# Sorted block attention into a maxout layer: item 1's query transposes from TensorE to DMA, later value loads, later steps

## The chip, the cores and the metric

The kernel runs on one core of a Trainium2 chip. The metric is the device time of one execution in microseconds (us). Times inside a profile are counted from the span's start; the span runs from the first to the last instruction of the program. In the profile TensorE is PE (its weight loads are PEld), VectorE DVE, ScalarE ACT, GpSimd POOL and SyncE SP.

## The reference

Four items (the batch), each with 8 heads of 768 tokens and head size 64. A head's keys and values are cut into 8 blocks of 96 tokens; a normalized 8 x 8 matrix P per head mixes ("sorts") the blocks; each query block attends to its sorted block; the heads side by side go through a maxout layer.

```python
P = sort_net
for _ in range(5):
    P = P - np.max(P, axis=-1, keepdims=True)
    P = np.exp(P)
    P = P / (np.sum(P, axis=-1, keepdims=True) + 1e-09)
    P = P / (np.sum(P, axis=-2, keepdims=True) + 1e-09)
k_sorted = np.einsum('bhij,bhjcd->bhicd', P, k_b).reshape(B, H, S, D)
v_sorted = np.einsum('bhij,bhjcd->bhicd', P, v_b).reshape(B, H, S, D)
scores = scale * np.matmul(q_b, k_sb.transpose(0, 1, 2, 4, 3))
scores = scores - np.max(scores, axis=-1, keepdims=True)
attn = np.exp(scores)
attn = attn / (np.sum(attn, axis=-1, keepdims=True) + 1e-09)
x = np.matmul(attn, v_sb)     # then the heads side by side: 3072 tokens x 512
out = np.maximum(x @ w1, x @ w2) @ w_out     # 512 -> 1024 -> 512
```

## The kernel before

All inputs are float32 in memory. GpSimd's DMA queue loads them and casts them to bf16 on the way. The maximum is rewritten: w1 becomes w1 - w2, the hidden part is a ReLU of x(w1 - w2), and the product of w2 and w_out, called wc (`w_product`, L654), is added by x. So an output tile of 128 tokens sums 12 matmuls of 512 columns: 8 on the hidden tiles g and 4 on xT.

**Stages.** Item 0's attention runs in a front part whose order is a written list (L777). Then, for each item b in turn, `units` are issued one after the other (L915 to L939): eight `moe_h` (hidden products, 4 for each half of the tokens), and twelve `moe_out` half-tiles of six matmuls, each pair of output tiles ending in one evacuation and one store of 512 KB on SyncE's queue. For item 0 the eight hidden units stand in the front, so its units 0 to 7 are empty, units 8 to 11 are the four `w_product`, and 12 to 23 are the output half-tiles. For items 1 and 2 units 0 to 7 are hidden and 8 to 19 output; item 3 has no attention beside it.

**Tails.** Next item's attention is laid between the units of the current one. The dictionaries `first_tail`, `second_tail` and `third_tail` (L859 to L913) say after which unit which steps are issued. Each engine runs its instructions in the order of issue, so a step that waits holds up all that follows it on its engine.

The steps of item b:
- KS, `sort_k` (L449), three of them: 32 small matmuls each sort keys into PSUM, then an evacuation to kT.
- `q_transposes` (L413), two halves of two head pairs each. For items 0 and 1, 24 TensorE transposes with the identity and one VectorE evacuation a half; for items 2 and 3, a DMA transpose on SyncE's queue out of q_pair, which `pair_q` (L403, two VectorE copies) makes from the loaded queries.
- SC, `scores` (L539), u = 0 to 7: eight matmuls and an exponential on ScalarE. u counts two halves of the blocks times four head pairs, so u = 0, 1, 4, 5 read half 0 of the turned queries and the others half 1.
- TURN, `turn_v` (L242): VectorE turns 24 of 96 columns of the loaded values into v_dc. The values of items 1 and 2 lie in two halves of the partitions and are turned and sorted together.
- VS, `sort_v_pair` (L516, eight of 16 matmuls, items 1 and 2) or `sort_v_halved` (L493, four, item 3, whose values lie in both halves): each reads all turned columns.
- VA, `values` (L567): eight matmuls, a reciprocal and a scaling on VectorE.
- TR, `x_transposes` (L600): for items 1 to 3 a DMA transpose on SyncE's queue, after two VA, into xT. The hidden products of token half 0 read TR0 (their first two matmuls) and TR1 (the next two), those of half 1 TR2 and TR3.

PSUM has four buffers of two banks, shared by all. `pick` (L96) gives an evacuation to ScalarE or VectorE by a running count of their loads, at build time.

**Loads.** All inputs but the small sort matrix are loaded on GpSimd's queue in order of issue; by the trace at most eight are under way, and the ninth waits for the first. The order before: item 0's values, keys, queries; the weights (L822 to L829); keys of 1 (L832), queries of 1 (L836), values of 1 and 2 in two pieces each (L837 to L839), keys of 2 (L840), queries of 2 (L844, into w2's place); values of 3 once turned values are out of v_raw (after unit 11 of item 0); keys and queries of 3 into v_raw's place (after unit 12 of item 1). A tiny GpSimd copy into `seen` (L771, L822) is used to hold that queue back until what it reads is there.

Of the kernel before, what the change touches and what calls it, by code (L numbers as in the profile page):

```python
# [11 lines left out]
BF16 = mybir.dt.bfloat16  # L12
# [4 lines left out]
def kernel(  # L17
# [16 lines left out]
    nc = tc.nc  # L34
# [12 lines left out]
    R = S // 128  # L47
    PB = 128 // NB
    HP = H // 2
# [5 lines left out]
    const = ctx.enter_context(tc.tile_pool(name="const", bufs=1))  # L55
# [60 lines left out]
    q_raw, qT = {}, {}  # L116
# [35 lines left out]
    def load_k(b):  # L152
        k_raw[b] = (
            kpool.tile([128, HB * D], BF16, tag="k_raw", name="k_raw")
            if b < 3
            else v_raw[:, 0 : HB * D]
        )
        n = HB * D // NCH
        for ci in range(NCH):
            nc.gpsimd.dma_start(  # L160
                out=k_raw[b][:, ci * n : (ci + 1) * n],
                in_=k_src[b, :, ci * n : (ci + 1) * n],
            )

    def load_v(b, pieces=2, which=None, half=None):
        r0 = (b % 2 if half is None else half) * 64
        n = BLK * D // pieces
        for m in range(pieces) if which is None else [which]:
            nc.gpsimd.dma_start(  # L169
                out=v_raw[r0 : r0 + 64, m * n : (m + 1) * n],  # L170
                in_=v_src[b, :, m * n : (m + 1) * n],
            )

    w1_sb = big.tile([128, HP, DFF], BF16, tag="w1", name="w1_sb")
    w2_sb = big.tile([128, HP, DFF], BF16, tag="w2", name="w2_sb")
# [222 lines left out]
    nc.vector.memset(v_sb[:, :, D : D + 1], 1.0)  # L398
    xT = big.tile([128, 2, 2, 2, 2, TCH], BF16, tag="xT", name="xT")

    q_pair = {}

    def pair_q(b, two):  # L403

# [8 lines left out]
    def q_transposes(b, half, eng=None):  # L413

        if half == 0:
            qT[b] = qpool.tile([128, HP, R, 128], BF16, tag="qT", name="qT")
        if b > 1:
            hps = slice(half * 2, half * 2 + 2)
            nc.sync.dma_start_transpose(
                out=qT[b][:, hps].rearrange("p h r c -> p (h r) c"),  # L420
                in_=q_pair[b][:, hps].rearrange("p h r d -> p (h r d)"),
            )
            return
        ps = ps_bf16("tq_ps")
        if b == 0 and half == 0:
            nc.tensor.matmul(
                ps[:, 0:128], fill[:, 0:128], ident, is_transpose=True, start=True, stop=True
            )
        for n in range(2 * R):
            hp, r = half * 2 + n // R, n % R  # L430
            c = slice(n * 128, (n + 1) * 128)
            for h2 in range(2):
                nc.tensor.matmul(  # L433
                    ps[h2 * 64 : h2 * 64 + 64, c],
                    q_raw[b][:, hp + 4 * h2, r * D : (r + 1) * D],
                    ident,
                    is_transpose=True,
                    start=True,
                    stop=True,
                )  # L440
        evac(
            qT[b][:, half * 2 : half * 2 + 2].rearrange("p h r c -> p (h r c)"),
            ps[:, 0 : 2 * R * 128],
            2 * R * 128,
            two_x=True,
            eng=eng,
        )
# [319 lines left out]
    turn_v(first, "A", 36, 56)  # L767
    turn_v(first, "A", 56, 80)
    block_diagonals_first()
    seen = const.tile([128, 2, 2], BF16, tag="seen", name="seen")  # L770
    nc.gpsimd.tensor_copy(out=seen[0:G, 0], in_=p_bf[:, NB - 1, NB - 2 :])  # L771
    load_w_columns(w2_sb, moe_w2, 0, 1)
    selections(1)
# [16 lines left out]
    def front_step(step):  # L790

        eng = step[-1] if step[-1] in "AD" else None
        name = step[:-1] if eng else step
        kind = name.rstrip("0123456789ab")
        n = [int(x) for x in name if x.isdigit()]
        if kind == "F":
            fills[0] = 512
        elif kind == "k":
            sort_k(0, n[0], 640 if step == front[0] else 0, eng)
        elif kind == "v":  # L800
            sort_v(0, n[0], 0, eng)
        elif kind == "tq":
            q_transposes(0, n[0], eng)
        elif kind == "SC":
            scores(0, n[0], fills_due())
        elif kind == "VA":
            values(0, n[0], fills_due())
        elif kind == "tx":
            x_transposes(0, n[0], eng)
        elif kind == "tw":  # L810
            w2_transposes(n[0], eng)()
        elif kind == "diff":
            w_difference(n[0])
        elif kind == "pe":
            block_diagonals([(0, 2), (0, 3), (1, 1), (1, 2), (1, 3)], 2)
        elif name[-1] == "a":
            moe_h_products(0, n[0], n[1], (0, 2), fills_due())
        else:
            moe_h(0, n[0], n[1], eng, (1, 3))
# [9 lines left out]
    load_w(wo_sb, moe_w_out)  # L829
    w_difference(0, nc.gpsimd)  # L830
    w_difference(1, nc.gpsimd)
    load_k(1)  # L832
    for step in front[1:-26]:
        front_step(step)

    load_q(1)  # L836
    for piece in range(2):  # L837
        for b in (1, 2):
            load_v(b, which=piece)  # L839
    load_k(2)  # L840

    for step in front[-26:]:
        front_step(step)
    load_q(2)  # L844
    load.update(A=600.0, D=300.0)

    def turn(rows, c0):
# [3 lines left out]
    def sorts_and_scores(b):  # L851
# [2 lines left out]

    SC, VA, TR, KS = sorts_and_scores(1)
    VS = [lambda t=t: sort_v_pair(2, t) for t in range(8)]
    TQ = [lambda half=half: q_transposes(1, half) for half in range(2)]
    TURN = [lambda c=c: turn(both, c) for c in (0, 24, 48, 72)]
    first_tail = {  # L859
        7: KS,  # L860
        9: [TQ[0], TURN[0]],
        10: [SC[0], TQ[1], TURN[1]],
        11: SC[1:4] + TURN[2:4] + [lambda half=half: load_v(3, half=half) for half in range(2)],
        12: VS[0:3],
        13: VS[3:6],
        14: VS[6:8] + [SC[4]],
        15: [VA[0], lambda: pair_q(2, 0)],
        16: [VA[1], lambda: pair_q(2, 1)],
        17: SC[5:8] + [TR[0]],
        18: [VA[2]],  # L870
        19: [VA[3], TR[1]],
        20: [VA[4]],
        21: [VA[5], TR[2]],
        22: [VA[6], VA[7], TR[3]],
    }
    SC, VA, TR, KS = sorts_and_scores(2)
    VS = [lambda t=t: sort_v_halved(3, t) for t in range(4)]
    TURN = [lambda c=c: turn(both, c) for c in (0, 24, 48, 72)]
    second_tail = {
        0: [lambda: q_transposes(2, 0), lambda: q_transposes(2, 1)],  # L880
        2: KS,
        4: SC[0:2],
        5: [VA[0]],
        6: SC[2:4] + [TURN[0]],
        7: [VA[1], TR[0]],
        8: [VA[2], TURN[1]],
        9: [VA[3], TR[1], TURN[2]],
        10: SC[4:7],
        11: [VA[4], TURN[3]],
        12: [VA[5], TR[2], lambda: load_k(3), lambda: load_q(3)],  # L890
        13: [VA[6]],
        14: SC[7:8] + VS[0:2],
        15: [VA[7], TR[3]],
        16: VS[2:4],
        17: [lambda: pair_q(3, 0)],
        18: [lambda: pair_q(3, 1)],
    }
    SC, VA, TR, KS = sorts_and_scores(3)
    third_tail = {
        0: [lambda: q_transposes(3, 0), lambda: q_transposes(3, 1)],  # L900
        2: KS,
        5: SC[0:2],
        6: [VA[0]],
        7: [VA[1], TR[0]],
        8: SC[2:5],
        9: [VA[2]],
        10: [VA[3], TR[1]],
        11: [VA[4]],
        12: SC[5:8],
        13: [VA[5], TR[2]],  # L910
        14: [VA[6]],
        16: [VA[7], TR[3]],
    }  # L913
    tails = [first_tail, second_tail, third_tail, {}]
    for b in range(B):  # L915
# [52 lines left out]
```

The softmax here doesn't subtract the row's maximum and nothing guards it: scores larger than these inputs give would overflow.

## Time and profile before

| | before |
|---|---|
| median of 3 runs | 166.89 us (166.74 to 166.93) |
| the profiled execution | 166.83 us |
| its span | 165.0 us, 4561 instructions |
| mean granted TensorE clock | 0.999 |
| hidden products, line L677 | 256 matmuls of 384 columns, 44.5 us busy |
| output products, line L704, on g and on xT | 46.0 and 24.7 us busy |
| DMA on GpSimd's queue (software_dynamic) | 13.37 MB, 50.0% of 16 engines' span |
| DMA on the hardware queues | 10.17 MB, 28.9% |
| HBM | 26.75 MB read, 6.29 MB written, 200 GB/s over the span |

The page gives each engine's busy time as a sum and in 40 slices of 4.1 us (a digit is tenths of a slice). The chain that ended last follows the last instruction back through whatever released each step; it tells where a shorter piece shortens the whole. Timelines merge equal instructions in order of time: start, length, engine, line, operation, output <- inputs, count, and in brackets how long the engine idled before and what ended it. In the table, as on the page, busy times of matmuls overlap, so they are larger than what a matmul adds.

### The profile page before, as it was taken

How to read it: one execution, taken by the hardware profiler on the slowest of the kernel's cores; microseconds unless marked ns; L12 is line 12 of the kernel's file. 1: busy time of each engine (PE TensorE's matmuls, PEld its weight loads, DVE VectorE, ACT ScalarE, POOL GpSimd, SP SyncE). 2: the span in 40 equal slices, each digit the busy share in tenths (PEclk: the TensorE clock that was granted, in tenths of full speed). 3: DMA queues.
4: the chain of work that ended last, by engine and by line, in shares of the span. 5: the costliest groups of instructions: out<-in, count | busy, mean ns of one | idle time of the engine just before them, and what ended most of it. 6: DMA issues, size and time to landing. Idle time of an engine off the chain costs nothing.

```text
span 165.0 us, 4561 instructions
## 1 busy us (share of the span) xinstructions
PE 157.0 (95%) x2007; PEld 95.4 (58%) x2025; DVE 77.5 (47%) x170; ACT 82.3 (50%) x101; POOL 33.9 (21%) x61
## 2 busy tenths in 40 slices
PE   7889999999999999999999999999999999999992
PEld 7839776756554555557655554575655546654451
DVE  4878995684366564525277763250642420000011
ACT  3489776617239846055652353457447206642020
POOL 7949997131206000000014010000000000000000
PEclk9999999999999999999999999999999999999999
DMA  3999999999999999689515999995025294000333
GB/s 41 204 204 194 164 196 207 209 205 220 210 203 204 220 224 167 175 84 228 111 19 104 126 212 157 200 309 29 0 52 175 50 164 142 0 0 0 127 131 127
DMA packets 30404, 23.90 MB, mean 145 GB/s; under 512 B 16752, under 2 KB 25200, under 8 KB 30384
## 3 DMA queue, kind: packets, MB, share of 16 engines
q0 software_dynamic: 11040, 13.37, 50.0%
q1 hardware_dynamic: 19200, 10.17, 28.9%
q8 instruction: 16, 0.26, 0.7%
q10 hardware_dynamic: 144, 0.07, 0.1%
q14 instruction: 4, 0.03, 0.1%
HBM read 26.75 MB, written 6.29 MB: 200 GB/s over the span
## 4 chain that ended last, share of the span: by engine, by line
PE 81%; DMA 6%; DVE 5%; ACT 3%; POOL 2%; issue 2%
PE out_ps L704 37%; PE h_ps L677 25%; DMA w_sb<-in_moe_w_dram 5%; PE wc_ps L657 4%; PE o_ps L575 4%; PE k_ps L458 3%; PE s_ps L548 3%; ACT e L556 1%; POOL w_sb L189 1%; PE v_ps L523 1%; DMA p_sb<-in_sort_net_dram 1%; PE tq_ps L433 1%; DVE colsum L276 1%; DVE p_sb L273 1%; PE tw_ps L638 1%
## 5 line engine op out<-in xcount | busy, mean ns | idle before, releaser
L704 PE MATMUL out_ps<-wo_sb,g 128*128 128x512 bf16 (+2 forms) x187 | 46.0, 370 | 1.4 <-issue 1.0
L677 PE MATMUL h_ps<-xT,w_sb 128*128 128x384 bf16 x256 | 44.5, 326 | 0.0
L677 PEld LDWEIGHTS <-w_sb 128*128 128x128 bf16 x256 | 24.0, 98 | 15.5
L556 ACT ACTIVATE e<-s_ps 96x768 bf16<-96x768 f32 x32 | 24.0, 805 | 14.8 <-PE s_ps L548 14.8
L691 ACT ACTIVATE g<-h_ps 128x768 bf16<-128x768 f32 x27 | 21.7, 811 | 17.4 <-PE h_ps L677 17.3
L704 PEld LDWEIGHTS <-g 128*128 128x128 bf16 x200 | 17.1, 97 | 15.8
L704 PE MATMUL out_ps<-wc,xT 128*128 128x512 bf16 (+2 forms) x98 | 24.7, 370 | 0.1
L108 ACT COPY o<-out_ps 128x1024 f32<-128x1024 f32 x10 | 10.1, 1012 | 28.0 <-PE out_ps L704 25.2
L592 DVE TENSOR_TENSOR x<-o_ps,rs 96x512 bf16<-96x512 f32 x32 | 22.0, 687 | 1.1
L704 PEld LDWEIGHTS <-xT 128*128 128x128 bf16 x100 | 9.6, 97 | 11.2
L575 PEld LDWEIGHTS <-e 96*128 96x128 bf16 x256 | 11.7, 97 | 5.7 <-DVE v_sb L110 0.2
L586 DVE RECIPROCAL rs<-o_ps 96x8 f32<-96x8 f32 x32 | 6.4, 201 | 17.2 <-PE o_ps L575 17.1
L739 DVE COPY o<-out_ps 128x512 f32<-128x512 f32 (+1 forms) x2 | 1.2, 625 | 27.6 <-PE out_ps L704 27.6
L575 PE MATMUL o_ps<-v_sb,e 96*128 96x65 bf16 x256 | 12.7, 193 | 0.0
L110 DVE CAST kT<-k_ps 128x1024 bf16<-128x1024 f32 x6 | 7.2, 1222 | 8.4 <-PE k_ps L458 8.4
L110 DVE CAST v_sb<-v_ps 96x1024 bf16<-96x1024 f32 x7 | 8.5, 1219 | 4.9 <-PE v_ps L523 2.2
L160 POOL DMA_DIRECT2D v_raw<-in_k_dram x3 | 2.5, 838 | 35.1 <-DVE v_dc L250 31.4
L108 ACT CAST v_sb<-v_ps 96x1024 bf16<-96x1024 f32 x9 | 8.8, 1015 | 1.6 <-PE v_ps L500 0.8
L169 POOL DMA_DIRECT2D v_raw<-in_v_dram x11 | 6.5, 593 | 12.7 <-DVE v_dc L250 6.4
L693 DVE TENSOR_SCALAR g<-h_ps 128x768 bf16<-128x768 f32 x5 | 4.8, 957 | 8.9 <-PE h_ps L677 8.8
L548 PEld LDWEIGHTS <-kT 64*128 64x128 bf16 x256 | 6.1, 94 | 4.8 <-issue 2.6
L548 PE MATMUL s_ps<-qT,kT 64*128 64x96 bf16 x256 | 8.5, 204 | 0.3 <-DVE qT L110 0.2
(97 smaller groups left out, 144.4 us busy)
## 6 DMA issues: line engine op xcount, KB each, us to landing
out_dram<-o SPq DMA_DIRECT2D x11, 512.0 KB, 3.4
v_raw<-in_v_dram POOLq DMA_DIRECT2D x8, 384.0 KB, 13.5
k_raw<-in_k_dram POOLq DMA_DIRECT2D x9, 256.0 KB, 11.0
w_sb<-in_moe_w_dram POOLq DMA_DIRECT2D x4, 256.0 KB, 6.0
w_sb<-in_moe_w_dram POOLq DMA_DIRECT2D x2, 512.0 KB, 9.6
wo_sb<-in_moe_w_out_dram POOLq DMA_DIRECT2D x2, 512.0 KB, 13.7
v_raw<-in_v_dram POOLq DMA_DIRECT2D x3, 256.0 KB, 5.0
q_raw<-in_q_dram POOLq DMA_DIRECT2D x4, 192.0 KB, 9.1
```

The lines of the kernel that those rows point to most:

```text
L108: nc.scalar.copy(out=out_ap, in_=in_ap)
L110: nc.vector.tensor_copy(out=out_ap, in_=in_ap)
L169: nc.gpsimd.dma_start(out=v_raw[r0 : r0 + 64, m * n : (m + 1) * n], in_=v_src[b, :, m * n : (m + 1) * n],)
L548: nc.tensor.matmul(ps[:, h2 * 512 + ii * 128 : h2 * 512 + ii * 128 + BLK], kT[b][rows, (hp * 8 + i) * BLK : (hp * 8 + i) * BLK + 128], rhs ...
L556: nc.scalar.activation(out=e[:, 0 : 8 * BLK].rearrange("p (t c r) -> p t c r", t=8, r=R), in_=ps[0:BLK] .rearrange("p (t f) -> p t f", t=8 ...
L575: nc.tensor.matmul(ps[:, h2 * 512 + ii * 65 : h2 * 512 + (ii + 1) * 65], e[:, (h2 * 4 + ii) * BLK : (h2 * 4 + ii) * BLK + 128], v_sb[:, m0 ...
L586: nc.vector.reciprocal(out=rs, in_=ov[:, :, :, 64])
L592: nc.vector.tensor_tensor(out=x, in0=ov[:, :, :, 0:D], in1=rs.to_broadcast([BLK, 2, 4, D]), op=ALU.mult,)
L657: nc.tensor.matmul(ps[:, 0:512], w2T[:, fb, dmt * 128 : (dmt + 1) * 128], wo_sb[:, fb, :], start=(fb == 0), stop=(fb == NFB - 1),)
L677: nc.tensor.matmul(h_ps[ch, t][:, m * 512 : m * 512 + TCH], w1_sb[:, hp, fb * 128 : (fb + 1) * 128], xT[:, b % 2, ch, hp % 2, hp // 2, :], ...
L691: nc.scalar.activation(out=g, in_=src, func=AF.Relu)
L704: nc.tensor.matmul(dst, g_tiles[b, ch, m // 2][:, m % 2, off : off + 128] if m < NFB else xT[:, b % 2, ch, hp % 2, hp // 2, off : off + 12 ...
```

## The change

The two halves of item 1's queries are turned by DMA transposes like those of items 2 and 3: `q_transposes` takes that branch for b > 0, and two `pair_q` copies are issued at the end of the front. Queries of item 1 are loaded ahead of its keys, both at the place where its keys were. A new function `hold_loads` lets GpSimd's queue wait until a half of an item's queries is turned; behind it now come the values of 1 and 2 in four pieces each, the queries of 2 and the keys of 2. The values of item 3 are issued in the second tail behind such a hold on item 2's queries, and each of their four DMAs takes every other run of 512 elements (1 KB in bf16) in place of one contiguous stretch. In the tails nearly all steps of attention move to later units; the two last value sorts of item 3 move into the third tail.

```diff
--- before.py
+++ after.py
@@ -166,10 +166,15 @@
         r0 = (b % 2 if half is None else half) * 64
         n = BLK * D // pieces
         for m in range(pieces) if which is None else [which]:
-            nc.gpsimd.dma_start(
-                out=v_raw[r0 : r0 + 64, m * n : (m + 1) * n],
-                in_=v_src[b, :, m * n : (m + 1) * n],
-            )
+            if half is None:
+                c = slice(m * n, (m + 1) * n)
+                dst, src = v_raw[r0 : r0 + 64, c], v_src[b, :, c]
+            else:
+                dst, src = (
+                    x.rearrange("p (k two x) -> p two k x", two=2, x=512)[:, m]
+                    for x in (v_raw[r0 : r0 + 64], v_src[b])
+                )
+            nc.gpsimd.dma_start(out=dst, in_=src)
 
     w1_sb = big.tile([128, HP, DFF], BF16, tag="w1", name="w1_sb")
     w2_sb = big.tile([128, HP, DFF], BF16, tag="w2", name="w2_sb")
@@ -398,7 +403,12 @@
     nc.vector.memset(v_sb[:, :, D : D + 1], 1.0)
     xT = big.tile([128, 2, 2, 2, 2, TCH], BF16, tag="xT", name="xT")
 
+    seen = const.tile([128, 2, 2], BF16, tag="seen", name="seen")
     q_pair = {}
+
+    def hold_loads(b, hp=HP - 1):
+
+        nc.gpsimd.tensor_copy(out=seen[:, 0], in_=qT[b][:, hp, R - 1, 126:128])
 
     def pair_q(b, two):
 
@@ -414,7 +424,7 @@
 
         if half == 0:
             qT[b] = qpool.tile([128, HP, R, 128], BF16, tag="qT", name="qT")
-        if b > 1:
+        if b > 0:
             hps = slice(half * 2, half * 2 + 2)
             nc.sync.dma_start_transpose(
                 out=qT[b][:, hps].rearrange("p h r c -> p (h r) c"),
@@ -767,7 +777,6 @@
     turn_v(first, "A", 36, 56)
     turn_v(first, "A", 56, 80)
     block_diagonals_first()
-    seen = const.tile([128, 2, 2], BF16, tag="seen", name="seen")
     nc.gpsimd.tensor_copy(out=seen[0:G, 0], in_=p_bf[:, NB - 1, NB - 2 :])
     load_w_columns(w2_sb, moe_w2, 0, 1)
     selections(1)
@@ -829,19 +838,24 @@
     load_w(wo_sb, moe_w_out)
     w_difference(0, nc.gpsimd)
     w_difference(1, nc.gpsimd)
-    load_k(1)
     for step in front[1:-26]:
         front_step(step)
 
     load_q(1)
-    for piece in range(2):
-        for b in (1, 2):
-            load_v(b, which=piece)
-    load_k(2)
+    load_k(1)
 
     for step in front[-26:]:
         front_step(step)
+    for half in range(2):
+        pair_q(1, half)
+    for half in range(2):
+        q_transposes(1, half)
+    hold_loads(1, 1)
+    for piece in range(4):
+        for b in (1, 2):
+            load_v(b, 4, which=piece)
     load_q(2)
+    load_k(2)
     load.update(A=600.0, D=300.0)
 
     def turn(rows, c0):
@@ -854,62 +868,68 @@
 
     SC, VA, TR, KS = sorts_and_scores(1)
     VS = [lambda t=t: sort_v_pair(2, t) for t in range(8)]
-    TQ = [lambda half=half: q_transposes(1, half) for half in range(2)]
     TURN = [lambda c=c: turn(both, c) for c in (0, 24, 48, 72)]
     first_tail = {
-        7: KS,
-        9: [TQ[0], TURN[0]],
-        10: [SC[0], TQ[1], TURN[1]],
-        11: SC[1:4] + TURN[2:4] + [lambda half=half: load_v(3, half=half) for half in range(2)],
-        12: VS[0:3],
-        13: VS[3:6],
-        14: VS[6:8] + [SC[4]],
-        15: [VA[0], lambda: pair_q(2, 0)],
-        16: [VA[1], lambda: pair_q(2, 1)],
-        17: SC[5:8] + [TR[0]],
-        18: [VA[2]],
-        19: [VA[3], TR[1]],
-        20: [VA[4]],
-        21: [VA[5], TR[2]],
-        22: [VA[6], VA[7], TR[3]],
+        9: KS,
+        10: SC[0:2],
+        11: SC[4:6],
+        12: SC[2:4] + [TURN[0]],
+        13: SC[6:8] + [TURN[1]],
+        14: [TURN[2]],
+        15: [TURN[3]],
+        16: VS[0:2],
+        17: VS[2:5],
+        18: VS[5:8],
+        19: [VA[0]],
+        20: [VA[1], TR[0]],
+        21: [VA[2], VA[3], TR[1]],
+        22: [VA[4], VA[5], TR[2]],
+        23: [VA[6], VA[7], TR[3]],
     }
     SC, VA, TR, KS = sorts_and_scores(2)
     VS = [lambda t=t: sort_v_halved(3, t) for t in range(4)]
     TURN = [lambda c=c: turn(both, c) for c in (0, 24, 48, 72)]
     second_tail = {
-        0: [lambda: q_transposes(2, 0), lambda: q_transposes(2, 1)],
+        0: [lambda: pair_q(2, 0), lambda: pair_q(2, 1)],
+        1: [
+            lambda: q_transposes(2, 0),
+            lambda: q_transposes(2, 1),
+            lambda: hold_loads(2),
+            lambda: load_v(3, half=0),
+            lambda: load_v(3, half=1),
+        ],
         2: KS,
-        4: SC[0:2],
-        5: [VA[0]],
-        6: SC[2:4] + [TURN[0]],
-        7: [VA[1], TR[0]],
-        8: [VA[2], TURN[1]],
-        9: [VA[3], TR[1], TURN[2]],
+        5: SC[0:2],
+        6: [VA[0]],
+        7: SC[2:4],
+        8: [VA[1], TR[0]],
+        9: [VA[2]],
         10: SC[4:7],
-        11: [VA[4], TURN[3]],
-        12: [VA[5], TR[2], lambda: load_k(3), lambda: load_q(3)],
-        13: [VA[6]],
-        14: SC[7:8] + VS[0:2],
-        15: [VA[7], TR[3]],
-        16: VS[2:4],
-        17: [lambda: pair_q(3, 0)],
-        18: [lambda: pair_q(3, 1)],
+        11: [VA[3], TR[1]],
+        12: [VA[4], TURN[0]],
+        13: [VA[5], TR[2], TURN[1]],
+        14: SC[7:8] + [TURN[2]],
+        15: [VA[6], TURN[3], lambda: load_k(3), lambda: load_q(3)],
+        16: [VA[7], TR[3]],
+        18: VS[0:2],
     }
     SC, VA, TR, KS = sorts_and_scores(3)
     third_tail = {
-        0: [lambda: q_transposes(3, 0), lambda: q_transposes(3, 1)],
-        2: KS,
-        5: SC[0:2],
-        6: [VA[0]],
-        7: [VA[1], TR[0]],
-        8: SC[2:5],
-        9: [VA[2]],
-        10: [VA[3], TR[1]],
-        11: [VA[4]],
-        12: SC[5:8],
-        13: [VA[5], TR[2]],
-        14: [VA[6]],
-        16: [VA[7], TR[3]],
+        0: VS[2:4] + [lambda: pair_q(3, 0)],
+        1: [lambda: pair_q(3, 1)],
+        2: [lambda: q_transposes(3, 0), lambda: q_transposes(3, 1)],
+        3: KS,
+        7: SC[0:2],
+        8: [VA[0]],
+        9: [VA[1], TR[0]],
+        10: SC[2:5],
+        11: [VA[2]],
+        12: [VA[3], TR[1]],
+        13: [VA[4]],
+        14: SC[5:8],
+        15: [VA[5], TR[2]],
+        16: [VA[6]],
+        18: [VA[7], TR[3]],
     }
     tails = [first_tail, second_tail, third_tail, {}]
     for b in range(B):
```

## The prediction

> **What bounds the kernel now.** I read the page first (busy shares, the forty slices, the chain that ended last), then the chain in order of time around item 1's attention, then timelines of TensorE, VectorE, GpSimd and SyncE, and last the DMA view of single issues, which gives each transfer's time to landing.
>
> ```profile
> PE 157.0 (95%) x2007; PEld 95.4 (58%) x2025; DVE 77.5 (47%) x170; ACT 82.3 (50%) x101; POOL 33.9 (21%) x61
> ...
> PE   7889999999999999999999999999999999999992
> ...
> DMA  3999999999999999689515999995025294000333
> ...
> PE 81%; DMA 6%; DVE 5%; ACT 3%; POOL 2%; issue 2%
> ```
>
> TensorE is nine tenths busy or more from the fourth slice on and carries 81% of the chain. So matmul time that goes is gained, unless a wait takes its place. The DMA row is as full as TensorE's for the first 66 us (16 slices of 4.1 us): loads can't be reordered freely there.
>
> ```profile
> 43.59 0.79 PE tq_ps L433 x24
> ...
> 46.49 0.79 PE tq_ps L433 x24
> ...
> 49.15 0.47 ACT wc L108
> ...
> 49.63 2.22 ACT e L556 x3
> ```
>
> In the chain in order of time (start, us, what), item 1's query transposes stand on TensorE's path twice. Three exponentials in a row then hold up the next value sorts.
>
> ```profile
> 45.69 0.82 DVE L250 COPY v_dc<-v_raw 128x768 uint32<-128x768 uint32 x1 [0.31 <-DMA v_raw<-in_v_dram]
> ...
> 49.48 1.58 DVE L250 COPY v_dc<-v_raw 128x768 uint32<-128x768 uint32 x2 [0.46 <-DMA v_raw<-in_v_dram]
> ```
>
> VectorE's timeline: the turns of items 1 and 2's values already start when those values land.
>
> ```profile
> q_raw<-in_q_dram POOLq DMA_DIRECT2D x1, 768.0 KB, 16.1
> ...
> qT<-q_pair SPq DMA_TRANSPOSE x4, 5.0
> ...
> v_raw<-in_k_dram POOLq DMA_DIRECT2D x1, 256.0 KB, 3.7
> xT<-x SPq DMA_TRANSPOSE x1, 7.6
> ...
> xT<-x SPq DMA_TRANSPOSE x1, 2.8
> ...
> DMA packets 2029, 4.22 MB, mean 211 GB/s; under 512 B 170, under 2 KB 1224, under 8 KB 2025
> ```
>
> Time to landing: item 1's queries (issued at 26.27); the existing query transposes; item 3's first key piece, alone; an output transpose issued at 89.19 beside key loads, and one at 69.02 in a quiet queue. Last, the loads' rate in 40:60 us.
>
> **What the Trainium skill says.** "DMA: Bandwidth & Descriptors", Queues, rings and completion order: each DMA engine takes its queues in turn, a packet at a time. So a transpose waits behind other queues' packets; 7.6 against 2.8 us agrees. The same page, DMA Transpose (X-bar), has a transpose next to ordinary DMAs need nothing for safety; the trace agrees that they overlap, but not for free. "TensorE: Matmul & The Clock Gate", Part 1, has the clock halve after about 3.4 us of idling; this trace has no such gap after the first slices (PEclk 9 throughout), so I only use it for a rival. "SBUF — State Buffer", Who interferes with whom: some vector copies block GpSimd's descriptor writing; item 3's value issue at 49.31, beside a turn, took 1.10 us against 0.53 for its neighbours.
>
> **The change part by part.**
>
> *Removed from TensorE.* 48 transposes: by the timeline 0.79 us from the first of a half to the next product, twice, 1.6 us. Small-row groups cost about 0.2 us a visit (matmul starts: 0.1 more on entering, 0.1 on leaving). The first tail has 8 visits before (keys 1, queries 1, scores with queries 1, scores 2, values 3 with scores in one) and 8 after (keys 1, scores 4, values 3), so with the visits kept about 1.45 us goes. The three-exponential hold-up goes too, since scores now come two at a time: 0.12 + 0.25 us in the matmul starts at 49.5 and 51.6. The second tail gets one visit more (+0.2, item 3's value sorts part from its last scores), and its wait of 0.16 us before item 2's scores at 79.02 goes, two units later. Sum: -1.8 us. Item 1's feed-forward block, at 70.94 before, would start at 69.1.
>
> *The DVE side.* Two PSUM evacuations of 0.96 go, two pair copies come (1.03 together at 105.10). VectorE idles from 37.8 until item 1's key sort, which covers them: nothing, if the queries land by about 41.
>
> *The new chain behind the queries.* Before, values were issued from 27.15 on and the queue never ran dry. Now no value is issued until half 0 of item 1's transposes has landed.
> 1. Queries now stand right behind the output weights, which land at 33.7 (19.23 + 14.4). Behind keys they took 4.9 us (37.5 to 42.4), for item 2 4.4 (52.7 to 57.1), in the first load 3.9. I take 38.3, ends 37.6 and 38.6.
> 2. Pair copies: 1.1, to 39.4.
> 3. Half 0's transpose: 5.0 alone. Keys, now second, have 1.3 to 2.5 us of loading left beside it. A smaller transpose beside loads took 5.3 (60.84) and 7.6 instead of 2.8. I add 1.3, ends 0 and 3: 45.7.
> 4. GpSimd's copy behind that wait: 0.2 to 0.3. Eight value issues, then item 2's queries and keys, queue behind it.
> 5. 1,573 KB of values in eight pieces (768 KB of bf16 per item): 3.7 for the first 256 KB, the rest at 211 GB/s 6.2: landed 55.9, with the ends of 1 and 3 and half 1's transpose beside it 54.3 to 58.8.
> 6. The fourth turn 0.82 and its semaphore: 56.8.
>
> The value sorts at unit 16 read all turned values. TensorE reaches them at 69.1 minus what follows: seven half-tiles of 1.30 (9.1), 128 sort matmuls at 18.5 ns and three visits (3.0), eight value products of 0.24 (1.9), so at 55.1. Wait: 1.6 us, ends 0 and 4. It absorbs smaller waits before it: item 1's keys land near 42 to 43.5, where TensorE gets to them at 41.7, and half 0 is needed at 45.2.
>
> *Output transposes closer to their user.* Now VA2, VA3 and TR1 stand at unit 21, two units before item 1's hidden products, which read TR1 after two matmuls. Before, the last value pair's matmuls ended at 69.65 and its transpose was issued at 71.39: 1.75 us of VectorE. Landing took 2.8 to 3.9. So TR1 lands 4.5 to 5.6 after VA3; from VA3 to the third hidden matmul it is two half-tiles, four value products and 0.33, 3.9 us. Wait 0.6 to 1.7. I take 1.2, as item 2's keys and an output store still load then (values end at 56; queries 4.4, keys 3.8 and two stores of 512 KB bring it to 66 to 67). Before, TR1 landed at 69.7 and had 1.3 us to spare.
>
> *Later steps.* Item 2's pair copies and transposes follow one unit into the next block, landing near 80.5, scores needed at 81.5. SyncE carries them behind TR3 and a store, as before. Item 3's values (four issues, now 1 KB packets, 1 MB by 3.7 + 1.3 MB/200 GB/s) are held to about 82 and land near 93; the first turn at unit 12 is at 94. A late one would block VectorE, with item 2's normalizations behind it. Item 3's keys and queries go on GpSimd behind the turns, the queries near 100 (94.62 before); at 8 to 10.5 us to landing, as before, 108 to 110.5. VectorE waits for them early in item 2's block, where TensorE has four PSUM buffers; its transposes land near 116 to 118, scores needed at 118. The third tail's transposes are two units later and still 1.4 us ahead of unit 4 of the last block. All nothing, with 1 to 2 us of cover each. The hold's GpSimd copies delay nothing else: that queue has only loads left. The smaller packets are priced within step 3's and these ends: between a gain of the turn-taking and a slower load (768 B queries at 160 to 180 GB/s).
>
> *Sum.* -1.8 + 1.6 + 1.2 = +1.0. The profiled execution took 166.83 us (span 165.0 and 1.8 around it); the median of 166.89 is 0.06 above. Forecast 167.9.
>
> **Rivals.**
> - *A, values in time (faster or level).* Steps 1 and 3 at their low ends give turned values by 55.1; then only TR1's 0.5 to 1.2 stands against 1.8: 165.9. For it: 6 KB value packets ran at 222 GB/s (item 3's, 57.1 to 64.2), and transposes alone take 5.0. Against: every step must be early; and the queue stands empty between keys and values.
> - *B, collision.* Transposes beside 2 KB key packets go as at 89.19: half 0 lands 3 us later than I take, keys late as well, and values start at 48 to 49: turned by 60, a wait near 5 us, maybe over the 3.4 us of the clock gate: 170.5. It decides from half 0 landing after 47.5.
> - *C, the main waits and a later one*: item 3's queries landing after 112 stop its scores: 169.
>
> **How the numbers follow.** Main case 0.50 (own range 167.2 to 169.5), A 0.26, B 0.16, C 0.08. About 0.2% (0.33 us) is what a measurement can tell here. Faster: 0.16 of A and 0.01 of main, 0.17. Same: 0.09 of A, 0.03 of main, 0.12. Slower: 0.71. The range runs from 165.8, into A, to 170.3, up to B's centre: about 0.1 left out on either side.
>
> **What would show it.** In the trace after: query transposes of item 1 on SyncE from about 39.4, the first landing near 45.7; GpSimd idle until then; the fourth turn near 56 with "DMA v_raw" as what ended its idling; a TensorE gap before the value sorts; a gap two matmuls into the next block. Wrong if the sorts follow unit 16 without one, or if the main gap is at item 1's keys or scores.

## The result and the profile after

The changed kernel takes 171.33 us in the median of four runs, against 166.81 for the kernel before; the ratio is 1.026 with a 95% interval of 1.022 to 1.031. The profiled execution took 170.99 us, its span is 169.2. Two of the four executions (171.67 and 173.31 us) show a mean granted TensorE clock of 0.990 where the other two have 0.999 and 1.000, and ratios here and below leave out executions that are over 1.5% longer than the fastest of their kernel (here 173.31), which medians keep.

The page of the changed kernel, in the parts that were shown of before (busy times, TensorE's and the DMA's slices, the chain by engine):

```profile
PE 156.2 (92%) x1959; PEld 94.0 (56%) x1977; DVE 78.0 (46%) x171; ACT 81.2 (48%) x100; POOL 38.6 (23%) x67
...
PE   7999998999999999899999999956899999999991
...
DMA  3999999999899995599599789959213465000332
...
PE 41%; DMA 36%; POOL 8%; DVE 8%; issue 3%; ACT 2%; SPq 0%; POOLq 0%; DVEq 0%
```

TensorE lost 48 matmuls and 0.8 us of busy time, and its row has a dent (5 and 6 tenths) in slices 27 and 28, which is 110 to 118 us. TensorE's share of the chain has fallen from 81% to 41%, and that of transfers has risen from 6% to 36%. The gaps themselves stand in TensorE's timeline of the changed kernel (start, length, and in brackets the idle time before with what ended it):

```profile
56.04 0.64 PE L533 MATMUL v_ps<-bd,v_dc 64*128 64x64 bf16 x32 [0.24 <-DVE v_dc L255]
...
70.81 3.73 PE L687 MATMUL h_ps<-xT,w_sb 128*128 128x384 bf16 x22 [0.55 <-DMA xT<-x]
...
103.02 1.46 PE L687 MATMUL h_ps<-xT,w_sb 128*128 128x384 bf16 x8
...
115.63 4.06 PE L687 MATMUL h_ps<-xT,w_sb 128*128 128x384 bf16 x24 [3.53 <-DVE kT L110]
...
120.15 0.51 PE L558 MATMUL s_ps<-qT,kT 64*128 64x96 bf16 x16 [0.46 <-DMA qT<-q_pair]
```

The kernel before has no idle time in item 2's block:

```profile
104.14 4.06 PE L677 MATMUL h_ps<-xT,w_sb 128*128 128x384 bf16 x24
...
109.77 4.07 PE L677 MATMUL h_ps<-xT,w_sb 128*128 128x384 bf16 x24
113.78 0.51 PE L548 MATMUL s_ps<-qT,kT 64*128 64x96 bf16 x16
```

The two waits that the prediction priced are small. At 103.02 item 2's hidden products start 1.1 us earlier than before (104.14), 0.6 of it owed to two value sorts that moved behind that point. All of the loss, and more, is in what follows: 3.53 us until VectorE evacuates item 3's sorted keys, and 0.46 us for item 3's turned queries. VectorE's timeline there, in the changed kernel:

```profile
113.42 1.03 DVE L417 COPY q_pair<-v_raw 128x1536 bf16<-128x1536 bf16 x2 [7.33 <-DMA v_raw<-in_q_dram]
114.36 2.35 DVE L110 CAST kT<-k_ps 128x1024 bf16<-128x1024 f32 x2
```

And in the kernel before:

```profile
105.10 1.03 DVE L407 COPY q_pair<-v_raw 128x1536 bf16<-128x1536 bf16 x2 [3.52 <-DMA v_raw<-in_q_dram]
108.87 2.36 DVE L110 CAST kT<-k_ps 128x1024 bf16<-128x1024 f32 x2 [2.74 <-PE k_ps L458]
```

In the changed kernel VectorE idles for 7.33 us in front of the copies of item 3's queries, and the evacuation that TensorE's PSUM buffers need stands behind those copies. Before, the copies were done 2.7 us ahead of the evacuation. The chain in order of time names the transfers that lead there:

```profile
75.00 5.32 DMA qT<-q_pair
...
83.04 10.72 DMA v_raw<-in_v_dram
...
99.42 13.98 DMA v_raw<-in_q_dram
...
114.51 5.60 DMA qT<-q_pair
```

They follow one another: item 2's query transposes let the hold go, item 3's values load, are turned and make room, item 3's keys and queries load, and its transposes follow. GpSimd's timeline shows what stands in front of the queries, first in the changed kernel, then in the kernel before:

```profile
95.01 4.43 POOL L160 DMA_DIRECT2D v_raw<-in_k_dram  x3 [11.31 <-DVE rs L596]
99.42 0.91 POOL L143 DMA_DIRECT2D v_raw<-in_q_dram  x1
```

```profile
84.30 0.58 POOL L160 DMA_DIRECT2D v_raw<-in_k_dram  x1 [31.39 <-DVE v_dc L250]
88.59 1.92 POOL L160 DMA_DIRECT2D v_raw<-in_k_dram  x2 [3.71 <-DVE rs L586]
94.62 0.89 POOL L143 DMA_DIRECT2D v_raw<-in_q_dram  x1 [4.11 <-DVE rs L586]
```

In the changed kernel three key pieces, 768 KB, are issued just ahead. By the times to landing they were down at 106.4, and the queries 7.0 us after that, at 113.4. In the kernel before the last key piece landed at 97.9 and the queries at 105.1, 7.2 us later. So one load of queries behind its keys takes as long as before; what is new is that all three key pieces now go just before it. Before, the first had landed at 88.0. From the queries' issue to their landing GpSimd's queue moved 1.50 MB in the changed kernel and 0.96 MB before (DMA view, 99.42:113.39 and 94.62:105.08).

Two accounts of this go into the experiments. Theory L: the late landing of item 3's queries, set by the chain of loads, is the loss. Its first rival D: the copies' place in VectorE's queue is the loss, and the queries would be nearly in time.

### The profile page after: what moved, and what is told of

The parts are those of the page before. It is cut to its first block, busy times and chain, and to the rows that moved or that the text cites. A ratio compares the mean times of both kernels' runs of the same rounds, so it can differ in the third digit from the quotient of the medians.

```text
span 169.2 us, 4474 instructions
## 1 busy us (share of the span) xinstructions
PE 156.2 (92%) x1959; PEld 94.0 (56%) x1977; DVE 78.0 (46%) x171; ACT 81.2 (48%) x100; POOL 38.6 (23%) x67
## 4 chain that ended last, share of the span: by engine, by line
PE 41%; DMA 36%; POOL 8%; DVE 8%; issue 3%; ACT 2%; SPq 0%; POOLq 0%; DVEq 0%
PE out_ps L714 22%; PE h_ps L687 12%; DMA v_raw<-in_v_dram 11%; DMA qT<-q_pair 9%; DMA v_raw<-in_q_dram 8%; DMA w_sb<-in_moe_w_dram 5%; POOL v_raw L177 3%; POOL v_raw L160 3%; PE o_ps L585 2%; DMA xT<-x 2%; POOL w_sb L194 1%; DVE q_pair L417 1%; PE v_ps L533 1%; PE s_ps L558 1%; DMA p_sb<-in_sort_net_dram 1%
## 5 line engine op out<-in xcount | busy, mean ns | idle before, releaser
L701 ACT ACTIVATE g<-h_ps 128x768 bf16<-128x768 f32 x29 | 23.3, 811 | 22.2 <-PE h_ps L687 22.0
L108 ACT COPY o<-out_ps 128x1024 f32<-128x1024 f32 x7 | 7.1, 1012 | 23.2 <-PE out_ps L714 17.8
L714 PEld LDWEIGHTS <-xT 128*128 128x128 bf16 x100 | 9.6, 97 | 11.2
L585 PEld LDWEIGHTS <-e 96*128 96x128 bf16 x256 | 11.4, 97 | 5.9 <-issue 0.4
L255 DVE COPY v_dc<-v_raw 128x768 uint32<-128x768 uint32 (+1 forms) x9 | 7.2, 809 | 6.9 <-DMA v_raw<-in_v_dram 5.8
L177 POOL DMA_DIRECT2D v_raw<-in_v_dram x15 | 8.5, 592 | 1.5 <-POOLq L972 0.8
```

The source lines that it names most:

```text
L108: nc.scalar.copy(out=out_ap, in_=in_ap)
L177: nc.gpsimd.dma_start(out=dst, in_=src)
L255: nc.vector.tensor_copy(out=dst.bitcast(U32).rearrange("p (d c) -> p d c", c=BLK)[:, :, c0:c1], in_=src.bitcast(U32).rearrange("p (c d) -> ...
L585: nc.tensor.matmul(ps[:, h2 * 512 + ii * 65 : h2 * 512 + (ii + 1) * 65], e[:, (h2 * 4 + ii) * BLK : (h2 * 4 + ii) * BLK + 128], v_sb[:, m0 ...
L701: nc.scalar.activation(out=g, in_=src, func=AF.Relu)
L714: nc.tensor.matmul(dst, g_tiles[b, ch, m // 2][:, m % 2, off : off + 128] if m < NFB else xT[:, b % 2, ch, hp % 2, hp // 2, off : off + 12 ...
```

## Experiments

Each is compared with executions of the kernel before that ran along with it on the same chip; their medians were 166.3 to 166.4. The diffs are against the changed kernel unless another is named.

**Key sorts ahead of the query copies.**

```diff
     third_tail = {
-        0: VS[2:4] + [lambda: pair_q(3, 0)],
-        1: [lambda: pair_q(3, 1)],
-        2: [lambda: q_transposes(3, 0), lambda: q_transposes(3, 1)],
-        3: KS,
+        0: VS[2:4],
+        3: KS + [lambda: pair_q(3, 0), lambda: pair_q(3, 1)],
+        4: [lambda: q_transposes(3, 0), lambda: q_transposes(3, 1)],
```

> Changed kernel, but in the third tail item 3's key sorts come ahead of the two copies that wait for item 3's queries (copies after unit 3, DMA transposes after unit 4). Theory L (the late landing of item 3's queries, 113.4 us, is the bound; the copies in front of the key evacuations only decide where TensorE meets it): the 3.5 us gap at item 2's hidden products goes, but a gap of some 4 us appears before item 3's first scores, whose turned queries still land near 120; time 170.5 to 171.5. Theory D (the blocked VectorE queue is the loss, the turned queries would be nearly in time): only about 0.5 us of wait before the scores is left, time 167 to 168.

Measured: 169.77 us, ratio 1.022 (1.016 to 1.028); the profiled execution 169.26. TensorE's timeline of this kernel:

```profile
118.46 0.51 PE L558 MATMUL s_ps<-qT,kT 64*128 64x96 bf16 x16 [2.23 <-DMA qT<-q_pair]
```

The 3.5 us gap is gone, and a wait of 2.23 us stands before item 3's first scores. Neither theory's figure was met. The queries landed at the same time (113.5) and most of the loss stayed, as L has it, but the transposes took 3.9 and 4.0 us to landing where they took 5.6 and 5.2 in the changed kernel. That made 1.7 us. Most of it is one stop: from 118.2 to 119.9 us the DMA engines moved 32 GB/s in the changed kernel, and this kernel has no such stretch while its transposes move. What stops them is left open.

**Item 3's queries apart from the turned values.**

```diff
-        if b == 2:
+        if b >= 2:
             t = w2_sb.rearrange("p t f -> p (t f)")[:, 0 : H * R * D].rearrange(
...
             lambda: load_v(3, half=1),
+            lambda: load_q(3),
...
-        15: [VA[6], TURN[3], lambda: load_k(3), lambda: load_q(3)],
+        15: [VA[6], TURN[3], lambda: load_k(3)],
```

> Changed kernel, but item 3's queries go to the place in w2 that item 2's queries have left, issued right behind item 3's values, so they no longer wait until item 3's values are turned. Theory L: the queries land before 100 us, both waits in item 2's block (3.5 and 0.5 us) go, item 3's first scores follow without a gap: time 166.5 to 167.5. Rival K (the whole load chain of item 3 is late, keys included, or the copies are late for another reason): the keys then stop the sorts near 108 us, gain under 2 us, time above 169.

Measured: 167.79 us, ratio 1.012 (1.010 to 1.015); the profiled execution 167.16. The queries landed at 100.9, and item 2's block runs through:

```profile
105.35 4.07 PE L685 MATMUL h_ps<-xT,w_sb 128*128 128x384 bf16 x24
109.36 1.71 PE L466 MATMUL k_ps<-bd,v_raw 64*64 64x64 bf16 x96
110.99 5.37 PE L685 MATMUL h_ps<-xT,w_sb 128*128 128x384 bf16 x32
116.30 0.51 PE L556 MATMUL s_ps<-qT,kT 64*128 64x96 bf16 x16
```

No bracket, no idle time. L holds: both waits hang on where the queries' load stands. The median is 0.3 us over the expected 166.5 to 167.5, for what is left here is the first part of the prediction: 1.12 us before the value sorts and 0.50 at item 1's hidden products.

**Item 3's keys apart instead**, in the buffer that item 1's keys have left; queries still behind the turns.

```diff
-        k_raw[b] = (
-            kpool.tile([128, HB * D], BF16, tag="k_raw", name="k_raw")
-            if b < 3
-            else v_raw[:, 0 : HB * D]
-        )
+        k_raw[b] = kpool.tile([128, HB * D], BF16, tag="k_raw", name="k_raw")
...
             lambda: load_v(3, half=1),
+            lambda: load_k(3),
...
-        15: [VA[6], TURN[3], lambda: load_k(3), lambda: load_q(3)],
+        15: [VA[6], TURN[3], lambda: load_q(3)],
```

> Changed kernel, but item 3's keys, not its queries, go to another place (the key buffer that item 1 has left), issued right behind item 3's values; the queries stay behind the turns. Theory Q (the 768 KB of keys issued just ahead of the queries are the 7 us that the prediction's step missed; the turns alone would have been in time): queries issued near 97 to 99 and landed by 107, both waits in item 2's block gone, time 167 to 168.5 as with the queries apart. Rival (the queries are late from the turns on, or slowed by transposes and stores whatever stands ahead): landed after 110, a wait of 1 us or more left, time 169 or more.

Measured: 166.95 us, ratio 1.004 (1.001 to 1.007); the profiled execution 167.36. The queries were issued at 100.13, no earlier than in the changed kernel, and took 9.8 us instead of 14.0: landed at 109.9. The first wait is gone, the one before the scores is 0.37 us. So the keys just ahead are what made the landing 4.2 us longer. It lies between the two theories' figures (107 and 110). An output transpose and a store run beside it (landed at 109.5 and 112.0); that they explain the rest of its lateness was not tested. The median is below that of the kernel with the queries apart although the profiled executions are 0.2 us apart the other way; that difference isn't explained.

**Turns on ScalarE.** Item 3's four turns are given to ScalarE.

```diff
-    TURN = [lambda c=c: turn(both, c) for c in (0, 24, 48, 72)]
+    TURN = [lambda c=c: turn_v(both, "A", c, c + 24) for c in (0, 24, 48, 72)]
```

> Changed kernel, but ScalarE instead of VectorE turns item 3's values. Item 3's three key issues took 2.15, 1.76 and 0.54 us on GpSimd beside VectorE's turns, where a quiet one takes 0.53. Theory G (vector copies hold up GpSimd's descriptor writing, and so the loads behind it): all three issues near 0.55 us, item 3's queries issued near 97 instead of 99.4 and landed 2 us or more earlier, time 168.5 to 169.5. Rival: the issues stay above 1 us, the queries land within 1 us of 113.4, time 170.5 to 172.

Measured: 172.96 us, ratio 1.027 (1.023 to 1.030), which stands on executions of 170.34 and 170.93; the profiled one took 174.99. In it the issues took 0.56, 0.55 and 0.54 us where they had taken 2.15, 1.76 and 0.54: vector copies did hold up GpSimd's issues. But ScalarE's turns ended later, the queries were issued at 101.4 and landed at 115.4, 13.9 us later, and the gap at the hidden products grew to 5.44 us. Part of the 13.9 belongs to this execution: from 105 to 109 us the DMA engines moved 58 GB/s, where the changed kernel has 164 in the like stretch (103 to 107), and why is open. So the trace can't be used against the keys, two of which were still under way at the issue, as in the kernel before. Of theory G the mechanism is shown and its gain is not there: 170.34 and 170.93 are no better than the changed kernel's 170.66 to 171.67. Whether shorter issues alone would gain was not tested, since the turns ended later with them.

**Item 3 put back to its old places.** The values of item 3 unheld after unit 15 of item 0, turns at 6 to 11, keys and queries at 12.

```diff
-        15: [TURN[3]],
+        15: [TURN[3], lambda: load_v(3, half=0), lambda: load_v(3, half=1)],
...
-            lambda: hold_loads(2),
-            lambda: load_v(3, half=0),
-            lambda: load_v(3, half=1),
...
+        6: [VA[0], TURN[0]],
+        8: [VA[1], TR[0], TURN[1]],
+        9: [VA[2], TURN[2]],
+        11: [VA[3], TR[1], TURN[3]],
+        12: [VA[4], lambda: load_k(3), lambda: load_q(3)],
...
+        14: SC[7:8] + VS[0:2],
+        16: [VA[7], TR[3]] + VS[2:4],
+        17: [lambda: pair_q(3, 0)],
+        18: [lambda: pair_q(3, 1)],
```

> Changed kernel with item 3's steps put back: its values issued after unit 15 of item 0 without a hold, turns after units 6 to 11 of item 1, keys and queries of 3 issued after unit 12, value sorts after 14 and 16, query copies after 17 and 18, third tail as in the kernel before. Item 1 as changed. Theory L: queries of 3 issued near 94 and landed by 106; no gap in item 2's block; item 1's part of the change is worth about 1 us: time 165.5 to 166.5. Rival T (without the hold, item 3's values load beside item 1's output transposes and delay item 1's hidden products): a gap of 2 us or more at item 1's first hidden products, time 167.5 or more.

Measured: 173.00 us, ratio 1.042 (1.039 to 1.045). Rival T's gap came true. TensorE's timeline, and below it the stages by engine with the granted clock (third column from the end):

```profile
75.11 5.18 PE L687 MATMUL h_ps<-xT,w_sb 128*128 128x384 bf16 x19 [5.06 <-DMA xT<-x]
```

```profile
70.00:75.00 5.00, 0.05 (x2) 0.00 (x0) 2.47 (x6) 0.61 (x1) 0.00 (x0) 0.72 1.31 169
75.00:78.00 3.00, 2.90 (x10) 1.37 (x11) 0.00 (x0) 0.08 (x1) 0.00 (x0) 0.50 1.12 308
```

Item 3's values load from 56 to 75 beside item 1's output transposes, TR1 lands after 7.6 us instead of 2.8, and TensorE waits for 5.06 us. From 75 to 78 us the clock is at 0.50, and 10 hidden products take 2.9 us where 22 took 3.73 in the changed kernel. Theory L's part on item 2's block came true, no gap is left there, though the queries landed only at 109.7, since the gap had moved all that follows. Without the gap and some 2 us for the slow clock 166 us would be left, an estimate from these figures, and that is L's time. The hold on item 3's values buys quiet transposes; taken away, it costs more than the late queries.

**Values of items 1 and 2 unheld**, on the kernel with the queries apart.

```diff
-    hold_loads(1, 1)
```

> As the kernel with item 3's queries set apart (167.8 us median, 167.2 profiled), without the hold in front of items 1 and 2's values: they are issued right behind item 1's keys, near 28 us. Theory H (loads and transposes in one set of DMA engines slow each other, and the hold is what gets item 1's queries turned in time): half 0 lands at 46 us or later instead of 42.9, TensorE waits 1 to 3 us before item 1's first scores (45.3), the wait before the value sorts (1.1 us) goes; time 167.5 to 169.5. Rival (the engines take turns, a transpose loses little beside 3 KB packets): half 0 lands by 45, both waits gone, time about 1 us less, 166.2 to 167.

Measured: 180.08 us, ratio 1.080 (1.076 to 1.084).

```profile
55.35 0.82 PE L556 MATMUL s_ps<-qT,kT 64*128 64x96 bf16 x16 [10.70 <-DMA qT<-q_pair]
```

H's direction, far beyond its 1 to 3 us. In the DMA view half 0's transpose, issued at 38.18, took 17.0 us to landing (4.3 in the changed kernel); it landed at 55.2, after all values (48.4) and after the queries of item 2 (54.1), which had been issued behind it. From 38.2 to 41 us none of its packets moved. From 44 to 55.2 us the DMA view has, by queue (packets, MB, share of 16 engines):

```profile
q0 software_dynamic: 1504, 1.78, 92.7%
q1 hardware_dynamic: 1505, 0.38, 27.3%
```

The first is GpSimd's loads, the second the two transposes. So the rival's premise holds, one packet of the transposes moved for each packet of the loads, but not its conclusion: a packet of a transpose has some 250 bytes here and one of a load some 1200 in the mean, and the transposes got 0.38 of 2.16 MB.

**Long runs for item 3's values.**

```diff
-            if half is None:
-                c = slice(m * n, (m + 1) * n)
-                dst, src = v_raw[r0 : r0 + 64, c], v_src[b, :, c]
-            else:
...
+            c = slice(m * n, (m + 1) * n)
+            dst, src = v_raw[r0 : r0 + 64, c], v_src[b, :, c]
```

> Changed kernel, with item 3's values in contiguous pieces (6 KB runs) in place of 1 KB runs; nothing else. If the short packets matter as they are placed here: values of 3 land over 1 us earlier than 93.8 and the output transpose issued near 86.7, which took 7.6 us, takes 9 or more. If they don't: both within 1 us, time within 1 us of the changed kernel's 171.0 to 171.7.

Measured: 169.99 us, ratio 1.023 (1.020 to 1.026). The values landed at 91.8 instead of 93.8, or 11.4 us after their first issue instead of 12.7, and the output transpose issued near 86 took 6.3 us, not 7.6. The first half of the expectation came true and the second went the other way: the 1 KB runs make the load longer and do not help the transpose beside it, whose first packet moved after 90 us in either kernel. In the ratio the two can't be told apart. The gap at item 2's hidden products was 2.98 us here, shorter than the 3.53 of the changed kernel, yet behind it the clock was at 0.50 from 116.4 to 118.4 us.

**Item 1's queries turned by TensorE again**, on the kernel with the queries apart.

```diff
-        if b > 0:
+        if b > 1:
...
+        8: [lambda: q_transposes(1, 0), loads_behind],
+        9: [lambda: q_transposes(1, 1)] + KS,
```

Here `loads_behind` is the hold and the loads after it, and the pair copies of item 1 are gone.

> As the kernel with item 3's queries set apart, but item 1's queries are turned by TensorE again (24 transposes after unit 8, 24 after unit 9; no pair copies), and GpSimd's hold waits for the VectorE evacuation of half 0. What the DMA transposes themselves are worth: TensorE's work grows by 1.5 us by the sum of the prediction; values are issued near 41.5 instead of 43.5, so the wait of 1.1 us before the value sorts goes. Net expected: 0.2 to 0.8 us slower than that kernel (168.0 to 168.6 median). If the saved TensorE time were not what carries: level or faster.

Measured: 168.14 us, ratio 1.013 (1.009 to 1.017); the profiled execution 168.17 against 167.16. The wait before the value sorts went, values were issued at 42.7, later than the 41.5 expected. The net of 0.4 us in the medians is inside the expectation, though the intervals overlap. So as the change is built, what the DMA transposes gain can't be told from the wait that they bring.

**Both waits taken out**, on the kernel with the queries apart.

```diff
-        16: VS[0:2],
-        17: VS[2:5],
-        18: VS[5:8],
-        19: [VA[0]],
+        17: VS[0:3],
+        18: VS[3:6],
+        19: VS[6:8] + [VA[0]],
...
+    def h_first():
+        moe_h_products(1, 0, 0, (0, 2))
+        moe_h_products(1, 0, 1, (0, 2))
+        moe_h(1, 0, 0, hps=(1, 3))
...
+        if b == 1:
+            units[0:2] = [h_first, h_second]
```

> As the kernel with item 3's queries set apart, with its two waits taken out: item 2's value sorts one unit later (3, 3 and 2 behind units 17, 18, 19; the last two before the first value product), and the first two hidden products of item 1 issued as in the front, both tiles' first halves before the second halves, so that TR1 is read 0.65 us of matmuls later and TR0 covers it. If these two waits are all that stands above: 1.1 and 0.5 us less than that kernel, 165.3 to 166.3, under the kernel before. If they only move (to the value products, or to item 1's later hidden products): 167 to 168.

Measured: 167.18 us, ratio 1.006 (1.004 to 1.008). Both gaps went and one came before the first value product, until ScalarE had evacuated the last value sorts. They only moved:

```profile
63.28 0.40 PE L583 MATMUL o_ps<-v_sb,e 96*128 96x65 bf16 x8 [1.78 <-ACT v_sb L108]
```

**The first value product one unit later**, beside the second (diff against the last kernel).

```diff
-        19: VS[6:8] + [VA[0]],
-        20: [VA[1], TR[0]],
+        19: VS[6:8],
+        20: [VA[0], VA[1], TR[0]],
```

> As the version with both waits taken out (167.2 us median), where a new wait of 1.8 us stood before the first value product, for ScalarE's evacuations of the value sorts; now that product goes one unit later, together with the second. If that wait is all that is left: 1.3 to 1.8 us less, 165.2 to 165.9, under the kernel before by 0.2 to 0.6%. If TR0 is now late for item 1's first hidden products, a gap there and 166.3 or more.

Measured: 165.79 us, ratio 0.997 (0.995 to 0.999): ahead of the kernel before, at the upper end of what was expected.

**The same with long runs for item 3's values.**

> As the last kernel, with contiguous pieces for item 3's values (6 KB runs). In the changed kernel these landed 2 us earlier and the transpose beside them 1.3 us sooner. Nothing waits for them here by the last traces: within 0.3 us of the last kernel. If the short runs still cost through the load chain behind them: 0.3 to 1 us less.

Measured: 165.53 us, ratio 0.995 (0.993 to 0.997). This is the best version here; from the one before it the intervals don't separate it. It is 0.9 us ahead of the kernel before (166.41), half of the 1.8 us that the prediction had TensorE gain. The only wait on another engine or a transfer that TensorE's timeline still shows in item 1's part:

```profile
64.03 0.65 PE L577 MATMUL o_ps<-v_sb,e 96*128 96x65 bf16 x16 [0.38 <-ACT v_sb L108]
```

Its chain is back at 81% TensorE and 6% DMA, as in the kernel before.

## Why the prediction was wrong

It forecast slower by 1.0 us; the kernel is slower by 4.5 (171.33 - 166.81; by the profiled executions 4.2), outside its range, and for another reason than the main case gave. The loss comes from the late queries of item 3, which it put at nothing. With those queries apart the kernel is still 1.5 us slower (167.79 against 166.29), near the 1.0 forecast. But the two waits left there are 1.12 and 0.50 us, not 1.6 and 1.2, and by the prediction's own sum a gain of 1.8 would make up for them; so that nearness is in part luck, and where the rest comes from is not shown.

- **TensorE's gain** was sized right. It put item 1's feed-forward block at 69.1 without waits. It started at 69.78. By the starts of the matmuls 0.3 to 0.4 us were lost before the value sorts and 0.31 before the value products, so without waits it stands near 69.1. The second of these, ScalarE's evacuations of the last value sorts, it had not seen.
- **Queries and copies** (steps 1 and 2): landed at 37.7, copied by 38.8; 38.3 and 39.4 were given.
- **Half 0's transpose** (step 3): 45.7 predicted, 43.1 measured. The 1.3 us added for the keys beside it was nothing; it took 4.25 us, less than the 5.0 taken for one alone.
- **Values** (step 5): 55.9 predicted, 55.1 measured, by an error the other way: 11.4 us from the first issue instead of 9.9. Step 6, turned at 56.0 instead of 56.8.
- **The wait before the value sorts**: 1.6 predicted, 0.24 in the profiled execution, 0.35 to 1.12 in the kernels that keep this part. **The wait at item 1's hidden products**: 1.2 predicted, 0.55 measured; TR1 took 2.8 us to landing, the low end.
- **"Later steps ... All nothing, with 1 to 2 us of cover each"** is the step that failed. Its term was item 3's queries "near 100 ... at 8 to 10.5 us to landing, as before". The issue was right (99.4); the landing took 14.0 us. The 10.5 was measured in the kernel before with a key piece already landed and two under way. The change issues all three keys just ahead, so that the latency of one DMA was carried over without the 768 KB now in front of it. What that cost TensorE are the waits of 3.53 and 0.46 us. The keys put apart took the landing to 9.8 us and left 0.37 us of wait, and the queries put apart removed both waits.
- **The cover** was missed too. The text has VectorE wait for the queries "early in item 2's block, where TensorE has four PSUM buffers", but not that the evacuations of item 3's keys are issued behind those copies. Each engine's order makes this readable from the diff: the copies after units 0 and 1, the key sorts after unit 3.
- **Rivals.** C named the queries landing after 112 as the point, and they landed at 113.4; but it had them stop the scores, at 169 with a chance of 0.08. It was not worked out from the load chain. B's collision did not happen in the changed kernel: the keys had landed by 41.5 and the hold kept the values back. Where the hold is gone, a collision with values cost 10.7 us. A's low waits were the nearer picture of the first part.
- **Two slips of the working** bear on nothing: in the kernel before item 2's scores start at 79.44, not 79.02, and item 3's values are four issues of 384 KB, so 1.5 MB and not 1 MB, which the sum beside it (a first piece and 1.3 MB more) has right.

## What to carry to other kernels

A transfer's time to landing belongs to its queue as much as to the transfer: before a latency is carried over, count the bytes that the change puts ahead of it, along the whole chain of holds and buffers freed. A wait for a late load should not stand in an engine's order ahead of an evacuation that TensorE needs. DMA transposes next to a full load queue get little of the engines, so they need quiet, and the hold that gives it to them has to be paid for in the loads behind.

## What the runs showed of the hardware

- A transpose of 384 KB took 4.3 us to landing beside the last key loads, and 17.0 beside a queue that stayed full. There the two queues moved 1504 and 1505 packets in the same 11.2 us, and the bytes went to the one with the larger packets. "DMA: Bandwidth & Descriptors", Queues, rings and completion order, in the Trainium skill has each engine take its queues in turn by packets. The equal counts agree with that.
- Beside a busy load queue the first packet of a transpose was late too: none moved in the first 2.8 us after the issue with the values unheld (38.2 to 41 us), nor in the first 3.3 us of the output transpose of the changed kernel (86.7 to 90 us). In a quiet queue such an output transpose had landed after 2.8 us. The reason is open.
- Gaps of 5.1 us and 5.4 us on TensorE were each followed by the granted clock at 0.50, for 4 to 5 us; after the 3.5 us of the profiled changed kernel it stayed at full speed, but after 2.98 us with the long runs it was halved. "TensorE: Matmul & The Clock Gate", Part 1, in the same skill has about 3.4 us as the window of idling, one that runs on freely. The two long gaps agree, the one of 2.98 us does not: the length of a gap alone doesn't tell here. Where it happens, a wait costs more than its length.
- GpSimd's issue of a 256 KB load took up to 2.15 us beside VectorE's turns and 0.56 with the turns on ScalarE. "SBUF — State Buffer", Who interferes with whom, in the same skill names copies among the VectorE operations that can block GpSimd's descriptor writing, and this agrees.
